# First expert: loads of the tokens' results get an earlier latest time in the list scheduler, and six high parts are cast by DMAs of GpSimd's queue

## The chip, the cores and the metric

The kernel runs on one core of one Trainium2 chip. The metric is device time in microseconds of one execution. All times are those of the profiled execution unless it is said otherwise; a line number such as L882 is a line of the kernel before.

## What is computed

Attention with a tanh cap over 2 x 12 heads of 448 x 64, and then two expert layers over the 896 tokens of 768 features, each with 2048 hidden features. The weights come as 64-bit floats, everything else is 32-bit.

```python
scores = cap * tanh((q @ k.T / sqrt(64)) / cap)
attn = softmax(scores) @ v                    # 2 x 12 x 448 x 64
x = attn.transpose(0, 2, 1, 3).reshape(896, 768)
h = x @ moe_w_in                              # 768 x 2048
g = where(h > 0, h, exp(min(h, 0)) - 1)
x = g @ moe_w_out                             # 2048 x 768
h = maximum(x @ moe2_w_in, 0)
out = (h * h) @ moe2_w_out
```

## The kernel before

**Precision.** Each matmul of 32-bit data is made of three in fp32r: high part by high part, high by low, low by high (`mm`, L487 to L489). So each operand exists twice: a high part, which is a cast, and a low part, which is the operand minus its high part.

**Weights.** SP loads them as 64-bit words into two buffers `raw0` and `raw1`, a couple of pieces at a time. `to_fp32` turns a couple into 32-bit floats in `f0` or `f1`: three ACT steps that read raw (L838, L837, L840), then two on DVE (L842, L844), and for the Strassen stages three more sums on DVE (L849, L852). `piece` then makes a piece's high part by a cast (L876 on ACT, or L877 on DVE, as the scheduler likes) and its low part by a subtraction on DVE (L882). The parts lie in slots: og0/og1, og2/og3, og4/og5 and og6/og7, and for some stages xh/xl; the even one is the high part.

**Stages of the first expert.** The hidden features are worked in four phases. In the first, products with `w_in` are plain (`plain_products`), the function of the hidden layer is made of the accumulators (`evac`: Relu L907, exp L913, L916, then the high and low parts gh and gl, L937 and L943), and six pieces of `w_out` follow (`out1_half`, pieces number 3 to 8, 24 matmuls each, their accumulators copied to yp at L1135). Then come Strassen products (`strassen_quad`), which also need sums of the tokens' blocks, yh and yl. These are made by `yp_sums`: the attention's results, which stand in DRAM as xd0 to xd5, are loaded into yp (L1247), DVE sums them (L1070) into the buffers ep0 to ep3, and high parts yh (L937 or L938) and low parts yl (L943) follow.

**What sets the order.** Attention is written out by hand. From its end on a list scheduler, `Plan`, orders the work, in two plans; the second covers both experts. Each task is added with its engines, a cost, what it reads and writes, and a lag for those who wait for it. PE's tasks keep their order. For each other task `run` works out a latest time backwards from PE's uses, and then each engine takes, among the tasks that are ready when it comes free, the one whose latest time is earliest. The engine queues then run in that order, and a queue whose next instruction waits holds up all that stands behind it. The plan knows of engines DVE, ACT and SP beside PE. The second plan doesn't know of the store of xd5 that attention's last task makes on SP, nor of the memory that yp takes over from attention's buffers.

Of the kernel before, what the change touches and what calls it, by code (L numbers as in the profile page):

```python
# [28 lines left out]
def attention_moe_kernel(  # L29
# [12 lines left out]
    nc = tc.nc  # L42
# [3 lines left out]
    P = 128  # L46
    NFULL = S // P
    LAST = S - NFULL * P
    KC = DM // P
    FC = DFF // P  # L50
    NP = H // 2
    KH = KC // 2
# [438 lines left out]
    def half(t, c, b):  # L491
        return t[:, b, c]

    PE, DVE, ACT, SP = "PE", "DVE", "ACT", "SP"

    def dve(n, fast=False):
        return 0.14 + n / (1920 if fast else 960)

    def act(n):
        return 0.17 + n / 1160  # L500
# [3 lines left out]
    class Plan:  # L504
# [2 lines left out]
        LAG = 0.15  # L507

        def __init__(self):
            self.tasks, self.writer, self.readers = [], {}, {}  # L510

        def add(self, options, reads=(), writes=(), lag=None):

            options = [options] if isinstance(options, tuple) else options
            i = len(self.tasks)
            before = set()
            for r in reads:
                if r in self.writer:
                    before.add(self.writer[r])
            for r in writes:  # L520
                if r in self.writer:
                    before.add(self.writer[r])
                before.update(self.readers.get(r, ()))
            before.discard(i)
            for r in reads:
                self.readers.setdefault(r, set()).add(i)
            for r in writes:
                self.writer[r], self.readers[r] = i, set()
            self.tasks.append((options, before, self.LAG if lag is None else lag))
# [8 lines left out]
        def run(self, free):  # L538
            tasks = self.tasks
            n = len(tasks)  # L540
            after = [[] for _ in tasks]
            for i, (_, before, _) in enumerate(tasks):
                for j in before:
                    after[j].append(i)
            latest, at = [0.0] * n, free[PE]
            for i, (options, _, _) in enumerate(tasks):
                if options[0][0] == PE:
                    latest[i] = at
                    at += options[0][1]
            for i in reversed(range(n)):  # L550
                options, _, lag = tasks[i]
                if options[0][0] != PE:
                    cost = min(o[1] for o in options)
                    latest[i] = min([latest[j] for j in after[i]] + [at + 5.0]) - cost - lag
            waiting = [len(before) for _, before, _ in tasks]
            ready = [0.0] * n
            pe = [i for i, t in enumerate(tasks) if t[0][0][0] == PE]
            queue = {PE: pe[::-1]}
            open_ = {e: [] for e in (DVE, ACT, SP)}

            def opened(i):
                for e, _, _ in tasks[i][0]:
                    if e in open_:
                        open_[e].append(i)

            for i in range(n):
                if not waiting[i]:
                    opened(i)
            order, left, done = [], n, set()
            while left:  # L570
                best = None
                for e in (PE,):
                    if queue[e] and not waiting[queue[e][-1]]:
                        i = queue[e][-1]
                        t = max(free[e], ready[i])
                        if best is None or t < best[0]:
                            best = t, e, i
                for e in (DVE, ACT, SP):
                    if open_[e]:
                        t = max(free[e], min(ready[i] for i in open_[e]))  # L580
                        if best is None or t < best[0]:
                            i = min(
                                (i for i in open_[e] if ready[i] <= t),
                                key=lambda i: (latest[i] + SHY * (e == DVE and len(tasks[i][0]) > 1), i),
                            )
                            best = t, e, i
                t, e, i = best
                options, _, lag = tasks[i]
                cost, fn = next((c, f) for o, c, f in options if o == e)
                if e in queue:  # L590
                    queue[e].pop()
                for q in open_.values():
                    if i in q:
                        q.remove(i)
                free[e] = t + cost
                for j in after[i]:
                    waiting[j] -= 1
                    same = all(o[0] == e for o in tasks[j][0])
                    ready[j] = max(ready[j], t + cost + (0.0 if same and e != SP else lag))
                    if not waiting[j]:  # L600
                        opened(j)
                order.append((t, i, e, cost, fn))
                left -= 1
            self.order = sorted(order, key=lambda o: (o[0], o[1]))
            for _, _, _, _, fn in self.order:
                fn()
            return free
# [24 lines left out]

    PLAIN = 0, 1
    OUT1 = ((0, 0), (1, 0), (0, 1), (1, 1), (2, 0), (2, 1))
    pieces = []
    for ph in range(PH):
        pieces += [
            (in_loads(w_in1, ph * QP + q, j), (ph, q) > PLAIN) for q in range(ph == 0, QP) for j in range(KH)
        ]
        pieces += [(out1_loads(ph, *at), False) for at in OUT1]  # L640
    for ph in range(PH):
# [18 lines left out]
    with tc.manual_schedule():  # L660
# [125 lines left out]
        plan = Plan()  # L786
        counts, slots = dict(piece=0, ep=0, set=1, made=0), list(OGS)
# [66 lines left out]

        def piece():

            k, z = place[counts["piece"]]
            full = couples[k][z][1]
            counts["piece"] += 1
            if k == counts["made"]:  # L860
                to_fp32()
            s = slots.pop(0)
            slots.append(s)
            if s < 4:
                h, l = groups[2 * s], groups[2 * s + 1]
                kh, kl = [("oh", s)], [("ol", s)]
            else:
                h, l = (t[:, 1, :KH].rearrange("p c n -> p (c n)")[:, :7 * P].rearrange(
                    "p (a n) -> p a n", n=P) for t in (xh, xl))
                kh, kl = ([(("x", kc, 1), p) for kc in range(KH)] for p in "hl")  # L870
            n = 7 if full else 4
            src = fs[(k + 1) % 2][:, z, 8 - n - (1 - full) * 4:8 - (1 - full) * 4]
            kf = [(x, k % 2, z) for x in ("f", "fx")]
            add(
                [
                    (ACT, act(n * P), lambda: nc.scalar.copy(h[:, :n], src)),  # L876
                    (DVE, dve(n * P, True), lambda: nc.vector.tensor_copy(h[:, :n], src)),  # L877
                ],
                kf, kh,
            )  # L880
            add(
                (DVE, dve(n * P), lambda: nc.vector.tensor_tensor(  # L882
                    l[:, :n], src, h[:, :n].bitcast(F32), op=ALU.subtract)),
                kf + kh, kl,
            )
            return h, l, kh + kl
# [301 lines left out]
        h, l = split_p_steps(end, 1)  # L1188
# [23 lines left out]
        made = [piece() for _ in range(KH - 1)]  # L1212
        plain_products(s1, range(1), made)
        to_fp32()
        free = plan.run({PE: 3.1, DVE: 2.1, ACT: 0.3, SP: 0.0})
        attn.close()
        gp = ctx.enter_context(tc.tile_pool(name="gp", bufs=1, side="right"))
        yh, yl = (gp.tile([P, 4, KH, S], F32R, name=x) for x in ("yh", "yl"))
# [7 lines left out]
        plan = Plan()  # L1226
# [5 lines left out]
        for ph in range(PH):  # L1232
            if ph:
                if ph == PLAIN[0] + 1:
                    slots.insert(0, 4)
                for q in range(QP):
                    if (ph, q) > PLAIN:
                        strassen_quad(next_set(), ph * QP + q, "elu")
                        continue
                    s = next_set()  # L1240
                    plain_products(s, range(KH))
                    plain_end(s, ph * QP + q, "elu")
            else:
                plain_products(s1, range(1, KH), made + [piece()])
                plain_end(s1, 1, "elu")
                for m in range(KC):
                    add((SP, 0.5, lambda m=m: nc.sync.dma_start(  # L1247
                        yp[:, m].rearrange("p (b s) -> p b s", b=B), xd[m])),
                        [("xd", m)], [("yp", m, b) for b in range(B)], 4.0)
                for j in range(KH):  # L1250
                    yp_sums(j)
            if ph == PH - 1:
                slots.remove(4)
            s = [next_set() for _ in range(KH)]
            for j, fp in OUT1:
                out1_half(s[j], fp)
                if fp:
                    out1_end(s[j], ph, j)
# [49 lines left out]
```

## Time and profile before

| | us |
|---|---|
| median of 3 runs | 569.45 (569.22 to 570.21) |
| the profiled execution | 571.93 |
| its span in the trace | 570.1 |
| PE busy | 561.3 |
| DVE busy | 484.8 |
| ACT busy | 405.7 |
| GpSimd (POOL) busy | 18.3 |

The granted TensorE clock is 1.00 of full speed, 2.4 GHz, in every stretch that was read. Attention ends at about 119 us, the plain products of the first phase of the first expert run to 144.8, the six pieces of `w_out` to 174.0, and Strassen stages follow. An engine's busy time says how much it worked; whether the end moves is read from what PE waits for, since PE is busy in 98% of the span. GpSimd has no work after attention.

### The profile page before, as it was taken

To read this page: it belongs to the slowest core of one execution; us is meant where nothing else is said; L and a number is where in the kernel's file an instruction comes from. 1 tells how busy PE (TensorE), PEld (TensorE's weight loads), DVE (VectorE), ACT (ScalarE), POOL (GpSimd) and SP (SyncE) were. 2 spreads that over 40 slices of the span, in tenths; PEclk is the share of its full clock that TensorE was granted. 3 is DMA by queue.
4 is the path that set the end of the run, shared out by engine and by line. 5 is a ranking of instruction groups with operands and counts; after the bars stand their busy time and mean duration, and the time that the engine had idled before them with its cause. 6 is when DMAs were issued, how large, how long until landed. Compare 5 with 4: busy or idle time off the path is not lost.

```text
span 570.1 us, 7830 instructions
## 1 busy us (share of the span) xinstructions
PE 561.3 (98%) x2940; PEld 491.4 (86%) x2940; DVE 484.8 (85%) x689; ACT 405.7 (71%) x445; POOL 18.3 (3%) x28
## 2 busy tenths in 40 slices
PE   8999999999998999999999999999999999999997
PEld 6777777689997999989999999998999899989985
DVE  6799999897899889989968995998889878987843
ACT  6889999955997994688537786696596369546700
POOL 3211011000000000000000000000000000000000
PEclk9999999999999999999999999999999999999999
DMA  7625444336754244424332333224423424332013
GB/s 188 172 68 158 122 128 142 104 123 212 242 179 129 94 139 156 139 77 158 104 115 75 115 111 144 75 75 148 143 91 124 160 76 135 126 110 74 2 66 129
DMA packets 65974, 70.20 MB, mean 123 GB/s; under 512 B 28544, under 2 KB 47872, under 8 KB 65936
## 3 DMA queue, kind: packets, MB, share of 16 engines
q1 hardware_dynamic: 64560, 69.05, 38.1%
q10 hardware_dynamic: 1344, 0.59, 0.4%
q8 instruction: 23, 0.38, 0.3%
q14 instruction: 15, 0.12, 0.1%
q0 software_dynamic: 32, 0.07, 0.0%
HBM read 64.09 MB, written 5.55 MB: 122 GB/s over the span
## 4 chain that ended last, share of the span: by engine, by line
PE 90%; DVE 6%; ACT 2%; issue 1%; DVEq 0%; ACTq 0%
PE acc L1112 20%; PE acc L489 18%; PE acc L487 18%; PE acc L488 18%; PE po L321 8%; PE sc L265 4%; PE pt L191 1%; DVE pl L297 1%; DVE ph L296 1%; PE sc L219 1%; ACT e L274 0%; DVE f L844 0%; DVE kql L215 0%; DVE yl L943 0%; DVE og L882 0%
## 5 line engine op out<-in xcount | busy, mean ns | idle before, releaser
L1112 PE MATMUL acc<-og,gh 128*128 128x512 f32 (+1 forms) x350 | 86.4, 338 | 0.0
L876 ACT CAST og<-f 128x512 fp32r<-128x512 f32 (+1 forms) x46 | 34.8, 766 | 58.1 <-DVE f L852 18.6
L838 ACT ACTIVATE f<-raw 128x1024 f16<-128x1024 f32 (+1 forms) x47 | 64.1, 1365 | 7.0 <-DMA raw<-in_moe_w_out_dram 3.4
L882 DVE TENSOR_TENSOR og<-f,og 128x512 fp32r<-128x512 f32 (+1 forms) x78 | 63.5, 831 | 5.1 <-ACT og L876 2.4
L489 PE MATMUL acc<-xh,og 128*128 128x448 f32 x180 | 66.2, 368 | 0.3
L1112 PEld LDWEIGHTS acc<-og,gh 128*128 128x128 f32 x350 | 60.3, 190 | 7.0
L488 PE MATMUL acc<-xl,og 128*128 128x448 f32 x180 | 66.0, 366 | 0.0
L487 PE MATMUL acc<-xh,og 128*128 128x448 f32 x180 | 65.9, 366 | 0.0
L487 PE MATMUL acc<-gh,og 128*128 128x448 f32 x176 | 64.5, 367 | 0.0
L488 PE MATMUL acc<-gl,og 128*128 128x448 f32 x176 | 64.5, 367 | 0.0
L489 PE MATMUL acc<-gh,og 128*128 128x448 f32 x176 | 64.5, 367 | 0.0
L840 ACT ACTIVATE f<-raw 128x1024 uint16<-128x1024 uint8 (+1 forms) x47 | 64.3, 1367 | 0.0
L1141 DVE TENSOR_TENSOR yp<-yp,acc 128x448 f32<-128x448 f32 (+2 forms) x69 | 43.4, 638 | 18.9 <-PE acc L1112 14.8
L1112 PE MATMUL acc<-og,gl 128*128 128x512 f32 (+1 forms) x175 | 59.2, 338 | 0.0
L844 DVE SCALAR_TENSOR_TENSOR f<-f 128x1024 uint32<-128x1024 uint32 (+1 forms) x47 | 56.8, 1209 | 1.4 <-ACT f L840 0.6
L837 ACT ACTIVATE f<-raw 128x1024 f32<-128x1024 f32 (+1 forms) x47 | 52.6, 1119 | 0.1
L274 ACT ACTIVATE e<-sc,tsc 128x896 f32<-128x896 f32 (+1 forms) x48 | 43.4, 908 | 0.2 <-PE sc L265 0.2
L487 PE MATMUL acc<-yh,og 128*128 128x448 f32 x112 | 41.4, 370 | 0.0
L489 PE MATMUL acc<-yh,og 128*128 128x448 f32 x112 | 41.0, 367 | 0.0
L488 PE MATMUL acc<-yl,og 128*128 128x448 f32 x112 | 41.0, 366 | 0.0
L297 DVE TENSOR_TENSOR pl<-e,ph 128x1792 fp32r<-128x1792 f32 (+1 forms) x24 | 37.6, 1566 | 1.9 <-DVE ph L296 0.5
L282 ACT ACTIVATE e<-e,capt 128x1792 f32<-128x1792 f32 (+1 forms) x24 | 38.6, 1608 | 0.8
(137 smaller groups left out, 1200.9 us busy)
## 6 DMA issues: line engine op xcount, KB each, us to landing
raw<-in_moe_w_in_dram SPq DMA_DIRECT2D x45, 512.0 KB, 4.4
raw<-in_moe_w_out_dram SPq DMA_DIRECT2D x48, 256.0 KB, 4.1
raw<-in_moe_w_out_dram SPq DMA_DIRECT2D x24, 512.0 KB, 4.3
bc<-far SPq DMA_DIRECT2D x12, 224.0 KB, 3.4
xd<-xn SPq DMA_DIRECT2D x12, 224.0 KB, 2.8
yp<-xd SPq DMA_DIRECT2D x6, 448.0 KB, 6.8
v<-in_v_dram SPq DMA_DIRECT2D x12, 192.0 KB, 3.3
k<-in_k_dram SPq DMA_DIRECT2D x15, 128.0 KB, 3.2
```

Of the source, the lines that this page charges most:

```text
L274: nc.scalar.activation(st["e", n][:, 2 * c:2 * c + w], st["sc", n, c][:, :w, :S], AF.Tanh, scale=tsc)
L321: nc.tensor.matmul(po[:, u, :S], vt[r, at[0]], pt[r, at[1]], start=i == 0 and j < 2, stop=i == 1 and j >= len(mms) - 2,)
L487: nc.tensor.matmul(acc, w[0], x[0], start=first, stop=False, skip_group_check=True)
L488: nc.tensor.matmul(acc, w[0], x[1], start=False, stop=False, skip_group_check=True)
L489: nc.tensor.matmul(acc, w[1], x[0], start=False, stop=last, skip_group_check=True)
L837: add((ACT, act(e) + 0.04 * n, lambda: nc.scalar.activation(a, hi, AF.Abs, scale=2.0 ** 16)), kr, ka)
L838: add((ACT, act(e) + 0.17 * n, lambda: nc.scalar.activation(top, hi, AF.Copy, scale=2.0 ** -100)), kr, kx)
L840: add((ACT, act(e) + 0.17 * n, lambda: nc.scalar.activation(bottom, byte, AF.Copy, scale=1 / 32, bias=-31 / 64)), kr, kx)
L844: add((DVE, dve(e), lambda: nc.vector.scalar_tensor_tensor(out=b, in0=b, scalar=3, in1=q.bitcast(U32), op0=ALU.logical_shift_left, op1=ALU ...
L882: (DVE, dve(n * P), lambda: nc.vector.tensor_tensor(l[:, :n], src, h[:, :n].bitcast(F32), op=ALU.subtract)),
L1112: nc.tensor.matmul(acc, x[:, f, g], w, start=a, stop=z, skip_group_check=True)
L1141: add((DVE, dve(n), lambda: nc.vector.tensor_tensor(to, to, acc(), op=ALU.add)), key + keys, keys)
```

## The change

Two things are changed, both in the stretch from about 130 to 180 us.

The loads of the tokens' results, yp<-xd, are added in another order (0, 3, 1, 4, 2, 5), and each gets an amount `soon` that is taken off its latest time: 30 for the first two, 15 for the next two, 0 for the last two.

For the six pieces of `w_out` in the first phase (`BY_DMA`, pieces 3 to 8), the cast to the high part is no longer a task of ACT or DVE but a DMA of GpSimd's queue, from f0 or f1 to the slot, with a type change on the way. The scheduler gets POOL as a further engine; it counts 0.6 us on the queue and 2.8 us until the cast has landed.

```diff
-                    latest[i] = min([latest[j] for j in after[i]] + [at + 5.0]) - cost - lag
+                    latest[i] = min([latest[j] for j in after[i]] + [at + 5.0]) - cost - lag - self.soon.get(i, 0.0)
...
-            open_ = {e: [] for e in (DVE, ACT, SP)}
+            open_ = {e: [] for e in (DVE, ACT, SP, POOL)}
...
+    BY_DMA = range(3, 9)
...
+            by_dma = counts["piece"] in BY_DMA
...
-            add(
-                [
-                    (ACT, act(n * P), lambda: nc.scalar.copy(h[:, :n], src)),
-                    (DVE, dve(n * P, True), lambda: nc.vector.tensor_copy(h[:, :n], src)),
-                ],
-                kf, kh,
-            )
+            if by_dma:
+                add((POOL, 0.6, lambda: nc.gpsimd.dma_start(h[:, :n], src)), kf, kh, 2.8 if n == 4 else 4.2)
+            else:
+                add(
+                    [
+                        (ACT, act(n * P), lambda: nc.scalar.copy(h[:, :n], src)),
+                        (DVE, dve(n * P, True), lambda: nc.vector.tensor_copy(h[:, :n], src)),
+                    ],
+                    kf, kh,
+                )
...
-                for m in range(KC):
+                for m in (m for j in range(KH) for m in (j, KH + j)):
+                    plan.soon[len(plan.tasks)] = 30 - 15 * (m % KH)
                     add((SP, 0.5, lambda m=m: nc.sync.dma_start(
```

The scheduler's other choices move with these two. Three places stand here; the others differ in kind no more than these. Lines behind the edit count six or seven higher in the new kernel: L907, L913, L916, L937 and L943 are L913, L919, L922, L943 and L949 there, L838, L837 and L840 are L840, L839 and L842.

On SP, at the end of attention's last work (xd5<-xn is its last store), before:

```order
L351 DMA far_1344<-rd_1343 64x14
L352 DMA bc_1345<-far_1344 64x896
L375 DMA xd5_100<-xn_1346 128x448
L655 DMA raw0_72<-in_moe_w_out_dram 128x2x128 x4
L655 DMA raw1_73<-in_moe_w_out_dram 128x2x128 x4
L1247 DMA yp_1510<-xd0_95 128x896
```

and now:

```order
L352 DMA bc_1345<-far_1344 64x896
L375 DMA xd5_100<-xn_1346 128x448
L1254 DMA yp_1510<-xd0_95 128x896
L1254 DMA yp_1510<-xd3_98 128x896
L657 DMA raw0_72<-in_moe_w_out_dram 128x2x128 x4
L657 DMA raw1_73<-in_moe_w_out_dram 128x2x128 x4
```

Two loads of yp stand ahead of the eight loads of weights that feed f1 (raw0) and f0 (raw1).

On ACT, where the hidden function of the last plain accumulators (acc4 to acc7) meets the couple of pieces 4 and 5 in raw0, before:

```order
L937 CAST gh_1504<-ep1_1507 128x896
L838 ACTIVATE f1_1331<-raw0_72 128x2x512
L837 ACTIVATE f1_1331<-raw0_72 128x2x512
L840 ACTIVATE f1_1331<-raw0_72 128x2x512
L907 ACTIVATE ep2_1508<-acc4_1462 128x448
L907 ACTIVATE ep2_1508<-acc5_1463 128x448
```

and now:

```order
L943 CAST gh_1504<-ep1_1507 128x896
L913 ACTIVATE ep2_1508<-acc4_1462 128x448
L840 ACTIVATE f1_1331<-raw0_72 128x2x512
L839 ACTIVATE f1_1331<-raw0_72 128x2x512
L842 ACTIVATE f1_1331<-raw0_72 128x2x512
L913 ACTIVATE ep2_1508<-acc5_1463 128x448
```

The Relu of acc4 moved ahead of the three steps on raw0.

On DVE, from gl of the first hidden features to og5, the low half of piece 4, before:

```order
L943 TENSOR_TENSOR gl_1505<-ep1_1507,gh_1504 128x896
L842 TENSOR_SCALAR f1_1331<-f1_1331 128x2x512
L844 SCALAR_TENSOR_TENSOR f1_1331<-f1_1331 128x2x512
L877 CAST og4_1332<-f1_1331 128x512
L882 TENSOR_TENSOR og5_1333<-f1_1331,og4_1332 128x512
```

and now, from the last of the four sums over yp on:

```order
L1076 TENSOR_TENSOR ep1_1507<-yp_1510,ep0_1506 128x448
L844 TENSOR_SCALAR f1_1331<-f1_1331 128x2x512
L944 CAST yh_1502<-ep0_1506 128x2x448
L846 SCALAR_TENSOR_TENSOR f1_1331<-f1_1331 128x2x512
L922 SCALAR_TENSOR_TENSOR ep2_1508<-ep2_1508,acc5_1463 128x448
L922 SCALAR_TENSOR_TENSOR ep2_1508<-ep2_1508,acc4_1462 128x448
L949 TENSOR_TENSOR yl_1503<-ep0_1506,yh_1502 128x2x448
L922 SCALAR_TENSOR_TENSOR ep3_1509<-ep3_1509,acc7_1465 128x448
L922 SCALAR_TENSOR_TENSOR ep3_1509<-ep3_1509,acc6_1464 128x448
L944 CAST gh_1504<-ep2_1508 128x896
L888 TENSOR_TENSOR og5_1333<-f1_1331,og4_1332 128x512
```

Four sums over yp (the first row is the last of them), a cast of yh and a subtraction of yl moved up here, the cast of og4 is no longer on DVE, a cast of gh came over from ACT, and og5 stands six instructions behind f1's last step, not two. On GpSimd, whose queue held nothing here, the six casts stand in the order of the pieces: og2, og4, og6, og0, og2, og4.

## Rows read from the trace of the kernel before

**Rows 1.** The page, part 1: busy us (share of the span) and instructions of each engine.

```profile
PE 561.3 (98%) x2940; PEld 491.4 (86%) x2940; DVE 484.8 (85%) x689; ACT 405.7 (71%) x445; POOL 18.3 (3%) x28
```

**Rows 2.** PE's waits, whole span: engine line <- releaser: us in total, times, longest us.

```profile
PE acc L489 <- DVE xl L882: 1.3, 1, 1.3
```

**Rows 3.** The timeline, PE, start of first Strassen stage: start us, us, engine line op.

```profile
174.22 0.36 PE L488 MATMUL acc<-xl,xh 128*128 128x448 f32 x1
175.85 0.47 PE L489 MATMUL acc<-xh,xl 128*128 128x448 f32 x1 [1.27 <-DVE xl L882]
176.16 0.36 PE L487 MATMUL acc<-xh,og 128*128 128x448 f32 x1
...
178.16 0.36 PE L487 MATMUL acc<-yh,xh 128*128 128x448 f32 x1
```

**Rows 4.** The timeline, PE: last plain products, then the first two pieces of w_out.

```profile
141.59 0.36 PE L489 MATMUL acc<-xh,og 128*128 128x448 f32 x1
...
144.83 0.36 PE L487 MATMUL acc<-gh,og 128*128 128x448 f32 x1
...
149.70 0.36 PE L487 MATMUL acc<-gh,og 128*128 128x448 f32 x1
...
150.10 0.37 PE L489 MATMUL acc<-gh,og 128*128 128x448 f32 x1
```

**Rows 5.** The timeline, ACT, 140 to 146 us.

```profile
140.80 1.39 ACT L838 ACTIVATE f<-raw 128x1024 f16<-128x1024 f32 x1
...
143.06 1.36 ACT L840 ACTIVATE f<-raw 128x1024 uint16<-128x1024 uint8 x1
144.29 0.93 ACT L907 ACTIVATE ep<-acc 128x448 f32<-128x448 f32 x2
```

**Rows 6.** The timeline, DVE, 139 to 176 us ([idle before <-releaser] at the end).

```profile
139.85 2.16 DVE L943 TENSOR_TENSOR gl<-ep,gh 128x896 fp32r<-128x896 f32 x2
143.19 0.69 DVE L842 TENSOR_SCALAR f<-f 128x1024 f32<-128x1024 f32 x1 [1.18 <-ACT f L837]
144.46 1.23 DVE L844 SCALAR_TENSOR_TENSOR f<-f 128x1024 uint32<-128x1024 uint32 x1 [0.58 <-ACT f L840]
...
146.18 0.69 DVE L882 TENSOR_TENSOR og<-f,og 128x512 fp32r<-128x512 f32 x1
...
148.99 1.15 DVE L916 SCALAR_TENSOR_TENSOR ep<-ep,acc 128x448 f32<-128x448 f32 x2
...
165.01 0.62 DVE L938 CAST yh<-ep 128x896 fp32r<-128x896 f32 x1
...
174.71 1.09 DVE L882 TENSOR_TENSOR xl<-f,xh 128x896 fp32r<-128x896 f32 x1
```

**Rows 7.** The timeline, DMA queue of SP, 132 to 148 us.

```profile
132.68 0.33 SPq L375 DMA_DIRECT2D xd<-xn  x1
133.05 4.05 SPq L655 DMA_DIRECT2D raw<-in_moe_w_out_dram  x8
137.28 0.52 SPq L1247 DMA_DIRECT2D yp<-xd  x1
...
145.38 2.52 SPq L1247 DMA_DIRECT2D yp<-xd  x5
```

**Rows 8.** DMA issues (131:145; then 143:152; then whole span): KB each, median us to landing.

```profile
raw<-in_moe_w_out_dram SPq DMA_DIRECT2D x10, 256.0 KB, 4.6
...
xd<-xn SPq DMA_DIRECT2D x1, 224.0 KB, 1.9
...
yp<-xd SPq DMA_DIRECT2D x5, 448.0 KB, 7.1
...
qz<-in_q_dram POOLq DMA_DIRECT2D x1, 64.0 KB, 2.8
```

**Rows 9.** Windows: us, busy of each engine, PEclk, DMA share, GB/s.

```profile
133.00:143.00 10.00, 10.00 (x51) 9.27 (x50) 7.13 (x12) 7.52 (x10) 0.00 (x0) 1.00 0.84 279
143.00:157.00 14.00, 14.00 (x71) 12.96 (x70) 12.96 (x20) 13.25 (x18) 0.00 (x0) 1.00 0.76 252
```

More of the change, by code (lines that the diff above doesn't have):

```diff
@@ L492, in half @@
         return t[:, b, c]
-    PE, DVE, ACT, SP = "PE", "DVE", "ACT", "SP"
+    PE, DVE, ACT, SP, POOL = "PE", "DVE", "ACT", "SP", "POOL"
     def dve(n, fast=False):
@@ L509, in __init__ @@
         def __init__(self):
-            self.tasks, self.writer, self.readers = [], {}, {}
+            self.tasks, self.writer, self.readers, self.soon = [], {}, {}, {}
         def add(self, options, reads=(), writes=(), lag=None):
@@ L577, in run @@
                             best = t, e, i
-                for e in (DVE, ACT, SP):
+                for e in (DVE, ACT, SP, POOL):
                     if open_[e]:
@@ L598, in run @@
                     same = all(o[0] == e for o in tasks[j][0])
-                    ready[j] = max(ready[j], t + cost + (0.0 if same and e != SP else lag))
+                    ready[j] = max(ready[j], t + cost + (0.0 if same and e not in (SP, POOL) else lag))
                     if not waiting[j]:
@@ L1214, in attention_moe_kernel @@
         to_fp32()
-        free = plan.run({PE: 3.1, DVE: 2.1, ACT: 0.3, SP: 0.0})
+        free = plan.run({PE: 3.1, DVE: 2.1, ACT: 0.3, SP: 0.0, POOL: 0.0})
         attn.close()
```

## Prediction

> **What bounds the kernel now.** Part 1 of the page comes first: PE is busy for 561.3 of 570.1 us [rows 1], so a change can give back only time in which PE waits. The list of PE's waits shows which of them this change can reach: most lie in attention, and one lies in the stretch that the second plan orders, 1.3 us of L489 on the DVE instruction that makes `xl` [rows 2]. The timeline of PE shows what it costs in all. L488 of the first Strassen product starts at 174.22, L489 only at 175.85, and the eighth matmul start after that L488 is at 178.16 [rows 3]. Eight steps took 3.94 us. Undisturbed, 24 steps take 149.70 - 144.83 = 4.87 us [rows 4], 0.203 each, so eight take 1.62: **2.3 us** are lost. The cause is DVE's queue, which reaches the subtraction into `xl` at 174.71 [rows 6], after PE wanted it. Earlier DVE stood idle: 1.18 and 0.58 us before the two steps on f1 at 143.19 and 144.46 [rows 6]. The change wants to fill such gaps with the sums over yp, and takes casts off DVE and ACT.
>
> **The profiled execution** took 571.93 us (span 570.1), 2.48 above the median of 569.45. I work out a difference on the trace and add it to both alike.
>
> **Part 1: the old wait.** From the end of f1's step at 144.46 + 1.23 = 145.69 DVE needs 29.0 us to reach `xl` at 174.71 [rows 6]. In the new order six, no longer ten, L1070 sums stand in that piece, the casts of og4, og6 and og0 are gone, one cast of yh goes to ACT, one subtraction of yl falls behind `xl`, and three casts or copies (gh, yp, xh) come over from ACT. With 0.62 for a cast of 896 [rows 6], about the same for a sum and a copy, 1.08 for one subtraction of 896 (half of the 2.16 at 139.85) and 0.49 for a small cast (it lay between 145.69 and the subtraction at 146.18), that is -4 x 0.62 - 3 x 0.49 - 0.62 - 1.08 + 3 x 0.62 = -3.8 us. So even if f1 is ready 2 us later, DVE reaches `xl` at about 173, ahead of PE. The 2.3 us go: **-2.3**.
>
> **Part 2: what is late next.** The second piece of w_out (og4, og5) is due on PE at 149.70, its low half og5 with the first L489 at 150.10 [rows 4]. Before, cast and subtraction followed f1 at once and the subtraction began at 146.18 [rows 6], 3 us early. Now three things stand in between, and I add them up.
>
> (a) ACT. The new order puts the Relu of acc4 ahead of the three steps on raw0. That bank's last matmul, the sixteenth before 144.83, starts at 141.59 and takes 0.36 [rows 4], so ACT, free at 140.80 before [rows 5], stands until 141.99 and spends 0.46 (half of 0.93) on it: the steps on raw0 start at 142.45, not 140.80. From the first one's start to the last one's end they took 143.06 + 1.36 - 140.80 = 3.62 us [rows 5]: end 146.07, 1.65 later than before.
>
> (b) SP. yp<-xd now stands twice ahead of raw0. yp takes the memory that attention leaves, and xd5's store reads from it, so SP waits for that store: issued at 132.68 [rows 7], landing 1.9 later [rows 8], 134.6. Two yp loads and four quarters of raw0 are then 2 x 0.459 + 4 x 0.262 = 1.97 MB; at 279 GB/s, the rate of this stretch [rows 9], 7.1 us: landed at 141.7, against 142.45 when ACT asks. No cost, with 0.7 us of margin. At the yp loads' own 7.1 us to landing [rows 8] it would be later than that.
>
> (c) GpSimd's DMA. f1's last step ends at 146.07 + 0.04 + 1.23 = 147.34 and the cast of og4 is issued at 147.4. How long such a DMA takes, no row shows: 262 KB, SBUF to SBUF, with a change of type, beside SP's loads. The bounds are 2.8 us (the one load from GpSimd's queue, 64 KB, in an almost idle start) and 7.1 us (yp<-xd, 448 KB, in these very microseconds) [rows 8]. I take the nearer row, GpSimd's own, 2.8, and add the other 0.197 MB at 252 GB/s [rows 9], 0.78 us, twice, because the engines are already 76% busy there with SP's transfers [rows 9]: **4.4 us**. og4 lands at 151.8, the subtraction takes 0.69 [rows 6], and L489 starts at about 152.55, not 150.10: 2.45 us, and 0.1 more as PE starts up again (from 175.85 to 176.16 the step was 0.31, not 0.20 [rows 3]): **+2.55**.
>
> The Trainium skill (DMA: Bandwidth & Descriptors, section Anatomy of one DMA — SWDGE (gpsimd) path) gives for a DMA of GpSimd's queue about 2.0 us and the bytes at 436 GB/s. For 262 KB that is an estimate from that page of 2.6 us; the sum would then end at the floor below, 569.2. No row here shows a cast by DMA, so the runs have to decide.
>
> A floor holds even for a fast DMA. Ahead of og5, DVE's queue now has ep2 twice (1.15 [rows 6]), yl (1.08), ep3 twice (1.15) and the cast of gh (0.62): 147.34 + 4.0 = 151.3, og5 ready at 152.0, L489 at 152.05, a loss of 2.05. Below that no speed of the cast leads.
>
> (d) Behind and beside. og3's subtraction waits for og2's cast, issued when PE has done with that slot, 48 matmuls or 9.7 us before 144.83 [rows 4], at 135.1, and landed at 139.5; DVE comes to it at 139.85, where gl stood [rows 6], and needs gl, two subtractions later, by 145.0. Hidden, but the two gl and four L1070 sums behind it (2.16 + 4 x 0.62) reach to about 145, and then two more instructions to 146.1, just when ACT is ready: an og2 that lands later than about 139.8 pushes f1 back by the same. A slow cast counts **twice**. The four casts that follow have more room: PE takes 4.87 us a piece, and each is issued over 5 us ahead of its use.
>
> Casts off ACT and DVE (six of about half a microsecond) are worth nothing by themselves: apart from the two places above PE waits for neither.
>
> **Sum.** -2.3 + 2.55 = +0.2 us: 572.1 on the profiled execution, **569.6** as a median.
>
> **Rivals.**
> *The cast is slow.* One mechanism: og2 late, so f1 late, then og4 late. L489 starts at 147.4 + 0.75 + L + (L - 4.6) for a cast of L us above 4.6. It is over 0.2% slower, stall over 3.4, from L = 4.9. At 5.5 it is 154.55: 4.45 + 0.1 - 2.3 = +2.2, **571.7**; at 7.1 it is 157.75, +5.4, 574.9. For it: yp<-xd at 7.1 beside it [rows 8]; against it: the 2.8 of GpSimd's own row, and a quarter of the engines' time idle. A late raw0 (b) adds its lateness to the same chain. Chance 0.3 with what goes with it.
> *The new wait is hidden* and the old one gone: 569.45 - 2.3 = **567.1**. It would need L489 by 150.10, so a cast under 1.9 us and none of the DVE rows ahead of og5. The floor speaks against it; it remains if ACT or DVE run ahead of what I read, or if the gaps in DVE are worth more than I see. Chance 0.1.
> *The change does not do what it says*, DVE is still late at `xl` and both waits stand: 569.45 + 2.5 = 572.0. PE reaches that place 2.5 us later itself, so this needs DVE to lose over 6 us. Chance 0.03, counted with the slow cast.
>
> **How the numbers follow.** The forecast, one wait for another, has 0.6; its own range is 569.2 (floor) to 570.5 (L near 4.9). About 0.2%, 1.1 us, is what a measurement of this kernel can tell from no change: 568.3 to 570.6 is the same. So faster 0.1, same 0.6, slower 0.3. The range leaves out the hidden wait and casts over 5.5 us: 568.7 to 571.8.
>
> **What would show it.** PE's waits: L489 on `xl` gone; a new wait of 2 to 2.6 us near 150 on og5's DVE line, at the first piece whose weights are og4 and og5. ACT's Relu of acc4 ahead of the steps on raw0, waiting for PE at about 141. GpSimd's DMAs with 3.4 to 5 us to landing. DVE's `xl` at about 173 with PE there at 176.5. I am wrong if og5 ends before 150, if raw0 lands after 142.5, or if the casts take under 3 or over 5 us.

## The result and the profile after

The changed kernel takes 576.49 us (median of 4 runs, 574.16 to 578.06) where the kernel before takes 569.83 (4 runs, 569.22 to 570.50): ratio 1.0113, 95% interval 1.0073 to 1.0154, so 1.1% slower. The forecast was 569.6 with a range of 568.7 to 571.8. The profiled execution took 578.06 us, its span is 575.9.

Pieces are counted from 0, as in `BY_DMA`: piece 3 is the first of w_out, piece 4 the second (the prediction's og4 and og5).

PE's waits, whole span (engine line <- releaser: us in total, times, longest): the old wait [rows 2] is gone, a longer one stands at the first product of piece 4.

```profile
PE acc L487 <- DMA og<-f: 5.1, 1, 5.1
```

The timeline of PE at that place, against [rows 4] (start us, us, engine line operation, [idle before <- releaser]):

```profile
143.67 0.36 PE L487 MATMUL acc<-gh,og 128*128 128x448 f32 x1
...
148.33 0.37 PE L489 MATMUL acc<-gh,og 128*128 128x448 f32 x1
153.79 0.71 PE L487 MATMUL acc<-gh,og 128*128 128x448 f32 x1 [5.09 <-DMA og<-f]
154.30 0.58 PE L488 MATMUL acc<-gl,og 128*128 128x448 f32 x1
154.67 0.58 PE L489 MATMUL acc<-gh,og 128*128 128x448 f32 x1
...
159.41 0.37 PE L487 MATMUL acc<-gh,og 128*128 128x448 f32 x1
```

Three losses are to be read here: 5.26 us beyond the usual step between 148.33 and 153.79; 0.31 as PE starts up again; and steps of 0.37 instead of 0.20 us until 159.1, about 2.3 us in all. The windows give the reason for the last (us, busy of PE, PEld, DVE, ACT and POOL, PEclk, DMA share, GB/s):

```profile
148.00:154.00 6.00, 0.91 (x5) 0.55 (x4) 2.37 (x5) 5.64 (x7) 0.00 (x0) 0.87 0.98 293
154.00:160.00 6.00, 6.00 (x18) 5.32 (x19) 5.97 (x9) 1.53 (x2) 1.04 (x2) 0.56 1.04 387
```

PE stood for 5.1 us, and behind that the granted clock was at half (1.2 instead of 2.4 GHz) for most of the second window; 18 matmuls ran where before, in the same window, it was 31.

Who made PE wait: the timeline shows when GpSimd's queue issues the casts and when SP issues its loads beside them, and the DMA issues of 144:150 say how long each took (KB each, median us to landing).

```profile
128.86 0.56 POOL L878 DMA_DIRECT2D og<-f  x1 [30.24 <-DVE f L846]
146.79 1.06 POOL L878 DMA_DIRECT2D og<-f  x2 [17.37 <-DVE f L846]
```

```profile
144.93 0.88 SPq L657 DMA_DIRECT2D raw<-in_moe_w_out_dram  x2
145.86 1.41 SPq L1254 DMA_DIRECT2D yp<-xd  x3
```

```profile
yp<-xd SPq DMA_DIRECT2D x3, 448.0 KB, 7.7
raw<-in_moe_w_out_dram SPq DMA_DIRECT2D x2, 256.0 KB, 3.1
og<-f POOLq DMA_DIRECT2D x2, 256.0 KB, 7.6
```

The cast of piece 3 was issued at 128.86, with much less beside it; the DMA issues of 126:140 have it:

```profile
og<-f POOLq DMA_DIRECT2D x1, 256.0 KB, 2.3
```

So the same 256 KB took 2.3 us there and 7.6 here; that is the median of two, the cast of piece 4 landed 6.9 us and the one of piece 5 8.3 us after its issue. That it was the company of SP's loads is what the experiments had to show.

### The profile page after: what moved, and what is told of

Its sections match the earlier page's. It is cut to its first block, busy times and chain, and to the rows that moved or that the text cites. A ratio compares the mean times of both kernels' runs of the same rounds, so it can differ in the third digit from the quotient of the medians.

```text
span 575.9 us, 7845 instructions
## 1 busy us (share of the span) xinstructions
PE 564.2 (98%) x2940; PEld 494.6 (86%) x2940; DVE 484.5 (84%) x687; ACT 403.2 (70%) x441; POOL 21.4 (4%) x34
## 4 chain that ended last, share of the span: by engine, by line
PE 94%; DVE 2%; ACT 2%; DMA 1%; issue 1%; POOLq 0%; ACTq 0%; DVEq 0%
PE acc L1118 20%; PE acc L487 19%; PE acc L489 19%; PE acc L488 19%; PE po L321 9%; PE sc L265 5%; PE pt L191 2%; DMA og<-f 1%; PE sc L219 1%; ACT e L274 0%; DVE pl L297 0%; DVE ph L296 0%; ACT e L282 0%; ACT f L840 0%; ACT f L842 0%
## 5 line engine op out<-in xcount | busy, mean ns | idle before, releaser
L882 ACT CAST og<-f 128x512 fp32r<-128x512 f32 (+1 forms) x44 | 33.5, 774 | 56.2 <-PE acc L488 17.8
L487 PE MATMUL acc<-gh,og 128*128 128x448 f32 x176 | 66.0, 375 | 5.1 <-DMA og<-f 5.1
L840 ACT ACTIVATE f<-raw 128x1024 f16<-128x1024 f32 (+1 forms) x47 | 64.2, 1366 | 6.8 <-DMA raw<-in_moe_w_out_dram 3.0
L489 PE MATMUL acc<-xh,og 128*128 128x448 f32 x180 | 66.1, 367 | 0.0
L487 PE MATMUL acc<-xh,og 128*128 128x448 f32 x180 | 66.1, 367 | 0.0
L488 PE MATMUL acc<-gl,og 128*128 128x448 f32 x176 | 65.8, 374 | 0.0
L489 PE MATMUL acc<-gh,og 128*128 128x448 f32 x176 | 65.7, 373 | 0.0
L842 ACT ACTIVATE f<-raw 128x1024 uint16<-128x1024 uint8 (+1 forms) x47 | 64.2, 1365 | 0.0
L839 ACT ACTIVATE f<-raw 128x1024 f32<-128x1024 f32 (+1 forms) x47 | 52.6, 1120 | 0.8 <-DVE og L888 0.8
L487 PE MATMUL acc<-yh,og 128*128 128x448 f32 x112 | 41.4, 370 | 0.0
L487 PEld LDWEIGHTS acc<-gh,og 128*128 128x128 f32 x176 | 33.8, 192 | 8.7 <-issue 5.4
L489 PE MATMUL acc<-yh,og 128*128 128x448 f32 x112 | 41.1, 367 | 0.0
```

Of the source, the lines that this page charges most:

```text
L487: nc.tensor.matmul(acc, w[0], x[0], start=first, stop=False, skip_group_check=True)
L488: nc.tensor.matmul(acc, w[0], x[1], start=False, stop=False, skip_group_check=True)
L489: nc.tensor.matmul(acc, w[1], x[0], start=False, stop=last, skip_group_check=True)
L839: add((ACT, act(e) + 0.04 * n, lambda: nc.scalar.activation(a, hi, AF.Abs, scale=2.0 ** 16)), kr, ka)
L840: add((ACT, act(e) + 0.17 * n, lambda: nc.scalar.activation(top, hi, AF.Copy, scale=2.0 ** -100)), kr, kx)
L842: add((ACT, act(e) + 0.17 * n, lambda: nc.scalar.activation(bottom, byte, AF.Copy, scale=1 / 32, bias=-31 / 64)), kr, kx)
```

## A sum that holds for all profiles

PE is busy in 98% of the span before [rows 1], so I split each span into three parts. **Gaps**: between 130 and 200 us, for each matmul step over 0.235 us, what it has beyond 0.203 (waits, restarts, half clock; in e6 also 24 added matmuls, 4.9). **Long step**: in stretches of some executions the step of the 128x448 matmuls is 0.2067 instead of 0.2027, at a granted clock that reads 1.00 for both; over such stretches 0.004 a step is summed. **Rest**: the span less both.

```
kernel                          span   gaps  long step  rest
before                          570.1   2.5     2.8     564.8
before again (e5)               567.7   2.4     1.9     563.5
after                           575.9   7.9     4.4     563.6
after again (e9)                573.7  10.1     0.0     563.7
e1 early loads only             568.9   2.2     2.5     564.2
e2 casts only                   572.4   8.2     0.7     563.5
e3 results' loads apart         573.5   6.1     3.8     563.7
e4 all loads apart              573.3   9.1     0.3     563.9
e6 no idle                      572.3   8.5     0.2     563.7
e7 pieces 4, 5 on engines       570.9   4.3     2.4     564.3
e12 the same again              573.5   7.1     2.6     563.8
e8 late casts only              570.6   4.7     2.5     563.4
e10 results' loads all early    569.3   4.6     0.7     564.0
e11 third piece only            569.7   2.8     3.0     564.0
```

The rest is 563.4 to 564.3 for thirteen of the fourteen, and 564.8 in the first profile of before, whose attention ended 1 us later than in the second. What the change does to the time is in the gaps of these 70 us; the long step comes and goes with the execution, in the kernel before as well.

## The experiments

The kernel before was run beside each group of experiments: its median was 569.15 us beside e1 to e4, 569.58 beside e5 to e8 and 570.51 beside e9 to e12. Each ratio is against those runs and is not the quotient of the two medians. Piece numbers are counted from 0, so "the fourth and fifth piece" of an expectation are pieces 4 and 5, but "the ninth piece" is piece 8.

**e1: the early loads alone.**

```
-    BY_DMA = range(3, 9)
+    BY_DMA = ()
```

> No high part is cast by a DMA; the lower latest time for the loads of the tokens' results is kept. Theory S (shared DMA engines: the cast of the fourth piece takes long because SyncE's loads run beside it; its lateness costs a wait of 5.1 us and then half the clock): without the casts the loads alone cost nothing, no wait on a DMA at the fourth piece, a wait for xl of 1 to 2 us is back; 568.5 to 570.0 us. Rival L (the moved loads are the cost, by holding up the raw loads or the queue): 573 us or more, with TensorE still late around 153. Open beside both: if the matmul pitch of 0.2067 from 159 on comes with the half clock, it is 0.2027 here until about 240, as before.

Measured: 568.68 us beside 569.15, ratio 0.9994 (0.9969 to 1.0019): no difference. The waits list has no DMA in this stretch, and a shorter old wait:

```profile
PE acc L489 <- DVE xl L888: 0.8, 1, 0.8
```

Theory L, the moved loads as the cost, falls.

**e2: the casts alone.** The loads of results as before the change:

```
-    for m in (m for j in range(KH) for m in (j, KH + j)):
-        plan.soon[len(plan.tasks)] = 30 - 15 * (m % KH)
+    for m in range(KC):
```

> Six high parts are cast by DMAs of GpSimd's queue, the loads of the tokens' results go where they went before the change. Theory S: the casts of the fourth and fifth piece are issued at about 146 beside two raw loads and all six loads of results (before: 252 GB/s in that stretch), land 6 to 8 us after issue, TensorE waits 3 to 5 us, the clock falls to 0.50 behind that; the wait for xl is gone; 572 to 575 us. Rival L (the moved loads are the cost): 567.0 to 569.0 us, the cast landing in 2.3 to 3 us.

Measured: 575.49 us, ratio 1.0104 (1.0060 to 1.0148), half a microsecond above theory S's range. Nearly the whole loss sits in the casts. DMA issues of 144:150, then PE's waits:

```profile
yp<-xd SPq DMA_DIRECT2D x5, 448.0 KB, 9.1
og<-f POOLq DMA_DIRECT2D x2, 256.0 KB, 8.1
```

```profile
PE acc L487 <- DMA og<-f: 4.2, 1, 4.2
```

**e3 and e4: the casts without the loads.** In e3 the last three loads of results wait for piece 5's low part (a one-column memset of each yp slice, which the load overwrites, holds them); in e4 the two raw loads of piece 8 as well (the lines that hold the loads; the rest of the edit is left out).

```
+    for m in (KH + 1, 2, KH + 2):                       # behind piece 5
+        add((DVE, 0.14, lambda m=m: nc.vector.memset(yp[:, m, :1], 0.0)),
+            pk, [("yp", m, b) for b in range(B)])
+        yp_load(m, 15 if m % KH == 1 else 0)
     elif k:
+        if k == 4:                                      # e4 only
+            add((DVE, 0.14, lambda: nc.vector.memset(
+                raw[:, 0, 0, :1].bitcast(U32), 0)), ends[0], kr)
         add((SP, 2.9 * n, load), [], kr, 1.5)
```

> As the changed kernel, but the last three loads of the tokens' results are made to wait for the fifth piece's low part, so that 1.4 MB less moves beside the casts of the fourth and fifth piece; the two raw loads still do. Theory S: some 1.5 MB instead of 2.9 MB at about 390 GB/s, the cast of the fourth piece lands 3.5 to 4.5 us after its issue instead of 6.8, the wait of 5.1 us falls to 1.5 to 3 us, and the time to 570.5 to 573.5 us. Rival V (the cast's own descriptors are late, because VectorE is busy then or because two casts stand in the queue): landing 6 us or more, wait about 5 us, 575 to 578 us.

> As the run before it, but the two raw loads of the ninth piece wait for the fifth piece's low part too: of SyncE's transfers none starts beside the two casts. Theory S: the two casts share the engines with each other alone, the first lands 2.3 to 4.4 us after issue, TensorE waits 0 to 2 us, the clock stays at 1.00; later waits for the delayed loads may take up to 1 us; 568.5 to 571.5 us. Rival V: landing 6 us or more, 575 to 578 us.

Measured: e3 575.59 us (573.07 to 576.76, 5 runs), e4 576.48. Both times lie above what theory S said (up to 573.5 and 571.5) and in theory V's range, so the totals alone would speak for V. The landings speak against it. DMA issues of e3 and of e4, 144:150:

```profile
raw<-in_moe_w_out_dram SPq DMA_DIRECT2D x2, 256.0 KB, 2.8
og<-f POOLq DMA_DIRECT2D x2, 256.0 KB, 2.4
```

```profile
og<-f POOLq DMA_DIRECT2D x2, 256.0 KB, 2.4
```

2.4 us in both (median of two casts), with VectorE at work in the same microseconds and two casts in the queue: theory V falls. In e3 the two raw loads still run beside the casts (they land at 147.7 and 148.4, the first cast at 149.2), so here it is the loads of results that stretch a cast to 7 or 8 us. Theory S had e3's landing at 3.5 to 4.5, too long. The timeline of PE in e3 shows what is left with a fast cast:

```profile
148.35 0.37 PE L489 MATMUL acc<-gh,og 128*128 128x448 f32 x1
149.35 0.44 PE L487 MATMUL acc<-gh,og 128*128 128x448 f32 x1 [0.63 <-DMA og<-f]
149.63 0.37 PE L488 MATMUL acc<-gl,og 128*128 128x448 f32 x1
150.85 0.47 PE L489 MATMUL acc<-gh,og 128*128 128x448 f32 x1 [0.86 <-DVE og L888]
```

Up to the L489 that is 1.9 us beyond the usual steps. Later e3 waits again, 1.0 us for the cast of piece 6 and 1.1 for a yl, and e4, whose raw data come late, for a low part (waits of e4):

```profile
PE acc L489 <- DVE og L892: 4.2, 3, 2.9
PE acc L487 <- DMA og<-f: 1.2, 1, 1.2
```

So in e4 the rivals' times can't be told by the total: its delayed loads cost what the early cast gave. e3's profiled execution took its median, 575.59; beside the second profile of before (569.53) it has 3.7 us more of gaps and 1.9 more of long step, which accounts for 5.6 of the 6.1 us. Whether its other executions had as much of the long step was not seen.

**e5: the kernel before, once more.**

> The kernel before, for a second profile of it. The pitch of the 128x448 matmuls (start to start) was 0.2027 up to about 243 and 0.2067 from there to about 370 in its first profile, 0.2027 from 185 on in the profile with the casts alone. Theory P (the longer pitch comes and goes with the execution, and makes the runs of one kernel differ by up to 3 us): another place or length of the stretch here, and the time goes with it: about 568.5 us without it, 571.5 us with 145 us of it. Rival Q (it belongs to the program): again from 243 to 370, 571 to 572 us.

Measured: 569.53 us (one run). Theory P holds: the long step is there, in another place. Two windows of this run; at the short step 40 us hold 199 or 200 matmuls, at the long one 195 or 196:

```profile
200.00:240.00 40.00, 40.00 (x195) 36.32 (x195) 36.13 (x53) 28.24 (x30) 0.00 (x0) 1.00 0.44 143
250.00:290.00 40.00, 40.00 (x200) 37.05 (x199) 38.15 (x58) 28.72 (x30) 0.00 (x0) 1.00 0.46 149
```

In the first profile of the same kernel the two windows are the other way round:

```profile
200.00:240.00 40.00, 40.00 (x199) 37.07 (x199) 36.81 (x54) 29.38 (x31) 0.00 (x0) 1.00 0.43 139
250.00:290.00 40.00, 40.00 (x196) 36.32 (x195) 37.60 (x57) 28.87 (x29) 0.00 (x0) 1.00 0.43 142
```

**e6: no idle time.**

```
+    for _ in range(24):     # into the bank that piece 4's first product overwrites
+        nc.tensor.matmul(bank(4 * s + 1), w[:, 0], gpart(gh, 0, 1),
+                         start=True, stop=True, ...)
```

> As the changed kernel, with 24 matmuls more (128x448, 24 times 0.2027 = 4.9 us) just ahead of the fourth piece's first product, into the bank that this product overwrites: TensorE works through the wait for the cast. Theory W (half the clock follows from the idle 5 us): the wait on the cast is under 1 us, the granted clock stays at 1.00 up to 165, the first product starts at about 154 as before, and the matmuls behind it come at 0.20 instead of 0.37 us: 2.6 us less, 573.5 to 574.5 us. Rival: the clock falls all the same (what lowered it isn't the idle time): 576 to 577.5 us.

Measured: 573.80 us (9 runs, 572.08 to 579.37), ratio 1.0086 (1.0058 to 1.0114). That is 4.2 above its own runs of before, where the changed kernel lay 6.7 and, in e9, 6.4 above its own: 2.2 to 2.4 us less, though the intervals overlap. PE's timeline:

```profile
149.24 5.23 PE L1053 MATMUL acc<-gh,og 128*128 128x448 f32 x24 [0.67 <-DVE ep L922]
156.51 0.47 PE L487 MATMUL acc<-gh,og 128*128 128x448 f32 x1 [2.05 <-DMA og<-f]
156.82 0.36 PE L488 MATMUL acc<-gl,og 128*128 128x448 f32 x1
```

The total lands as theory W put it, and the clock too: granted 1.00 from 148 to 165, steps of 0.20 behind the first product. That product starts 2.7 us later than in the changed kernel, since raw0 landed later in this execution (ACT waited 2.31 us for it), and PE still waits 2.05 us for the cast where theory W had under 1. So that the total agrees is partly luck; what this profile shows is that with 2.05 us of idle time in place of 5.09 the half clock didn't come.

**e7 and e12: the casts of pieces 4 and 5 back on the engines.**

```
-    BY_DMA = range(3, 9)
+    BY_DMA = 3, 6, 7, 8
```

> As the changed kernel, but the casts of the fourth and fifth piece (those that land beside the loads, and whose f is ready last) go to ScalarE or VectorE again; the other four stay DMAs. Theory S: the wait of 5.1 us and the half clock are gone, waits of up to 0.7 us at the fourth and fifth piece on the engines' casts and 1.5 us on xl stay: 568.5 to 570.5 us. Rival: the four other casts cost too (each holds its product by its own latency): 572 us or more.

> The kernel with the casts of the fourth and fifth piece on the engines again: its gaps between 130 and 200 were 1.8 us above those of before, its median 4.5 us. Theory G: gaps of 4 to 5 us again and 571 to 573 us, the first median having been raised by executions with a long stretch of the 0.2067 pitch. Rival: gaps of 6 us or more in this execution, the casts of the sixth to eighth piece landing later, and 573.5 to 575 us again.

Measured: 574.13 and 574.01 us, ratios 1.0083 and 1.0053. Theory S of e7 expected 568.5 to 570.5; its rival, that the four other casts cost too, had 572 or more and was right, and so was e12's rival (gaps of 6 us or more, 573.5 to 575). PE's waits in this stretch, of e7 and of e12:

```profile
PE acc L489 <- DVE xl L888: 1.6, 1, 1.6
PE acc L487 <- DVE ep L922: 0.6, 1, 0.6
```

```profile
PE acc L489 <- DVE xl L888: 2.5, 1, 2.5
PE acc L487 <- DVE ep L922: 1.1, 1, 1.1
```

No DMA is waited for, and the 5.1 us are gone, as expected. But the old wait is longer than before (1.3 [rows 2]), and it differs by 0.9 us between two executions of one kernel; in e12 the half clock came behind it, gaps 7.1 instead of 4.3. Some executions of these kernels pay more than one profile shows. What makes DVE late at `xl` can be read from its timeline: the low parts of pieces 6 and 7 wait in its queue for the casts by DMA, which were issued at about 155 and landed 5.2 to 6.8 us later (e7, then e12):

```profile
160.17 0.69 DVE L888 TENSOR_TENSOR og<-f,og 128x512 fp32r<-128x512 f32 x1 [1.89 <-DMA og<-f]
161.59 0.69 DVE L888 TENSOR_TENSOR og<-f,og 128x512 fp32r<-128x512 f32 x1 [0.73 <-DMA og<-f]
```

```profile
160.30 0.69 DVE L888 TENSOR_TENSOR og<-f,og 128x512 fp32r<-128x512 f32 x1 [1.78 <-DMA og<-f]
162.43 0.69 DVE L888 TENSOR_TENSOR og<-f,og 128x512 fp32r<-128x512 f32 x1 [1.44 <-DMA og<-f]
```

That is 2.6 and 3.2 us of DVE's time. It reaches `xl` at 176.54 and 177.28, where e1, with no cast by DMA, reaches it at 173.96: 2.6 and 3.3 us later. So a cast by DMA holds up not only PE but also DVE, through the subtraction that stands behind it in DVE's queue.

**e8: two late casts only**, on the kernel before (loads of results as in e2, `BY_DMA = 6, 7`).

> The kernel before with one thing changed: the casts of the sixth and seventh piece alone (counted from 0: numbers 6 and 7) go as DMAs of GpSimd's queue, the loads of results as before. VectorE or ScalarE is rid of 2 casts ahead of the wait for xl (1.3 us long before), TensorE needs these pieces only after 160. Theory S (a cast by DMA pays where its operand is ready early): the wait for xl falls below 0.5 us, no wait on a DMA: 567.0 to 569.0 us, 0.1 to 0.4% less than before. Rival: their landing of 4.4 us beside the raw loads of that stretch makes the product wait, 569.5 to 571 us.

Measured: 571.75 us, ratio 1.0031 (1.0015 to 1.0046). The rival was right in kind (its upper end was 571): the two casts landed after 6.6 us (median), beside raw loads of 512 KB, and PE waits for the first of them, DVE 3.2 us for the same one, while the wait on `xl` shrinks by 0.2 only:

```profile
PE acc L489 <- DVE xl L888: 1.1, 1, 1.1
PE acc L487 <- DMA og<-f: 0.9, 1, 0.9
```

**e9: the changed kernel, once more.**

> The changed kernel, for a second profile. Theory G (span = a base equal in all these kernels, plus TensorE's gaps between 130 and 200, plus what the longer pitch costs; the ten profiles so far give a base of 562.5 to 563.9 us): gaps of 7 to 9 us again (a wait of 4.5 to 6 us for the fourth piece's cast, the clock at 0.50 for some 6 us behind it), pitch in another place; span 563.3 + gaps + pitch within 1 us. Rival: the gaps differ by more than 2 us from execution to execution (the cast's landing depends on how the loads' packets fall), so that one profile doesn't speak for the median of 576.5 us.

Measured: 576.95 us beside 570.51, ratio 1.0116. The wait is 6.7 us this time, the cast landed after 8.4, the clock was at 0.50 behind it (waits; DMA issues of 144:150; window):

```profile
PE acc L487 <- DMA og<-f: 6.7, 1, 6.7
```

```profile
og<-f POOLq DMA_DIRECT2D x2, 256.0 KB, 8.4
```

```profile
154.00:160.00 6.00, 4.28 (x12) 3.76 (x13) 4.39 (x6) 1.84 (x3) 0.00 (x0) 0.50 0.88 311
```

Theory G's sum holds; so does its rival's point, gaps 2.2 us larger than in the first profile.

**e10: all loads of results early.**

```
-    plan.soon[len(plan.tasks)] = 30 - 15 * (m % KH)
+    plan.soon[len(plan.tasks)] = 30
```

> As the changed kernel, but all six loads of the tokens' results get the lowest latest time (30 us off for each), so that the last three go out at about 139 instead of 146 and nothing but the two raw loads runs beside the casts of the fourth and fifth piece. Theory S: these casts land in 2.2 to 3.0 us instead of 6.8 to 7.6, TensorE waits 0.5 to 1.2 us for the fourth piece's cast and up to 0.9 us for its low part, the clock stays at 1.00, no wait for xl; gaps of 3 to 4.5 us: 570.0 to 573.0 us. Rival: the four loads ahead of the seventh piece's raw loads make those late: a new wait on an f, 574 us or more.

Measured: 571.73 us, ratio 1.0039 (1.0012 to 1.0066): with all six casts still DMAs, moving three loads from 146 to 137 to 139 gives back 5.2 of the 6.4 us that e9 lost beside the same runs of before. DMA issues of 144:150 and waits:

```profile
raw<-in_moe_w_out_dram SPq DMA_DIRECT2D x2, 256.0 KB, 4.2
og<-f POOLq DMA_DIRECT2D x2, 256.0 KB, 4.1
```

```profile
PE acc L487 <- DMA og<-f: 3.1, 2, 2.5
```

The time and the clock, 1.00, are as theory S said. The landing, 4.1, lies above its 2.2 to 3.0, and the wait for the cast of piece 4, 2.5, above its 0.5 to 1.2: the loads of results now stand ahead of the last four quarters of the raw loads, which landed up to 149.0, and two more raw loads followed up to 146.5, so some of SP's loads still ran beside the casts.

**e11: the cast of piece 3 only** (`BY_DMA = 3,`).

> As the changed kernel, but of the six casts only the first stays a DMA (piece 3, issued at about 129 and landed 2.3 us later with no load beside it, its product at 145). Theory S (a cast by DMA costs nothing where its operand is ready well ahead): like the early loads alone (568.7 us), plus up to 0.6 us at the fourth piece: 568.3 to 570.0 us. Rival F (every kernel with casts on GpSimd's queue pays a fixed 2 us or more, whatever their place, as the median of 574.1 us with four casts suggests): 570.5 to 572.5 us.

Measured: 571.28 us beside 570.51, ratio 1.0001 (0.9969 to 1.0034). The median lies in F's range, but the runs of before beside it are 1.4 us longer than those beside e1, and against them F's 2 us (1.0035) lie just outside the interval; so this speaks for theory S, by a small margin. The old wait is gone here, and the time not: a wait at piece 4 has come in its place.

```profile
PE acc L487 <- DVE ep L922: 1.0, 1, 1.0
```

No version here is faster than the kernel before; e1 and e11 equal it.

## Why the prediction was wrong, step by step

**Part 1, the old wait goes:** right in its effect, wrong in its reason. DVE was to reach `xl` at about 173; it reached it at 177.35, since it stood for the casts itself, 3.63 us ahead of the subtraction at 153.68 and 1.14 us for the cast of piece 6. The working took three casts off DVE and had no term for DVE waiting for them. The wait is gone because PE comes later still, at 181.5.

**(a) ACT and f1:** right. The timeline of ACT has the Relu of acc4 first, with the wait for PE that was forecast, then the steps on raw0:

```profile
140.83 0.54 ACT L913 ACTIVATE ep<-acc 128x448 f32<-128x448 f32 x1 [1.33 <-PE acc L489]
141.27 1.39 ACT L840 ACTIVATE f<-raw 128x1024 f16<-128x1024 f32 x1
```

In this execution attention ended 1.16 us earlier (143.67 against 144.83 [rows 4]), so 141.27 answers to 142.43; 142.45 was forecast. DVE's last step on f1 and the subtraction behind the cast:

```profile
144.94 1.23 DVE L846 SCALAR_TENSOR_TENSOR f<-f 128x1024 uint32<-128x1024 uint32 x1
...
153.68 0.69 DVE L888 TENSOR_TENSOR og<-f,og 128x512 fp32r<-128x512 f32 x1 [3.63 <-DMA og<-f]
```

f1 ends at 146.17, which answers to 147.33; 147.34 was forecast.

**(b) the early loads cost nothing:** right in the total, by e1, and ACT doesn't wait for raw0 above. But the margin was smaller than the 0.7 us of the forecast: raw0's last quarter landed at 141.04, 0.2 us before ACT read it, and in e4, e11, e12 and e6 ACT waited 0.5 to 2.3 us for raw0.

**(c) the cast's landing is the step that failed.** Forecast 4.4 us; the cast of piece 4 was issued at 146.79, 0.6 us behind f1 where 0.06 was reckoned, landed 6.9 us later, and let the first product start at 153.79. In e9 it landed after 8.1. The lower bound of 2.8 was too high for a cast with little beside it (2.3), the upper one of 7.1 too low for e9, and the choice between them was wrong: the load from GpSimd's own queue was the nearer row by queue, the load of results the nearer one by place and time. The working counted the company as a share of engine time (76% busy) and added 0.78 us for it. A better count takes all bytes that are in flight together: two raw loads, three loads of results and two casts, 2 x 0.262 + 3 x 0.459 + 2 x 0.262 = 2.4 MB from 144.93 on; at the 293 GB/s of the window they end 8.3 us later, at 153.2. That is a reckoning after the event, and its agreement with the landing at 153.7 is partly luck, since it counts transfers that landed behind it (the second cast at 155.6, the last load at 155.8). But e3, e4 and e10 move the same way: with fewer bytes beside it the cast lands earlier. The Trainium skill (DMA: Bandwidth & Descriptors, section Anatomy of one DMA — SWDGE (gpsimd) path) gave an estimate of 2.6 us: it is near the casts with little beside them, 2.3 and 2.4, and far from those beside the loads of results, 6.9 to 8.1.

The place of the wait was wrong too: the forecast had PE wait at the first L489, for og5. But the first L487 reads og4 itself, due at 149.70 and by the forecast's own landing, 151.8, not there; that is where PE waited.

What (c) cost in all is 7.9 us where 2.55 was forecast: 5.26 of wait, 0.31 of starting up, and 2.3 of half clock, for which the forecast had no term.

**The floor for a fast cast,** a loss of 2.05 us through DVE's queue, held in the main: e3 lost 1.9 up to that L489, and there DVE came to og5 at 150.11, when the cast had landed at 149.21.

**(d) a slow cast counts twice:** wrong. Piece 3's cast was issued at 128.86, not 135.1, as its f and its slot were free by then, and no one waited for it. So the rival "the cast is slow" had the direction and the long landing, but its 574.9 us at 7.1, 5.4 above before, came from a second delay that didn't happen, while the one that did had no term: the half clock behind an idle PE, 2.3 us in the first profile and 2.5 in the second. That 5.4 is also the difference of the gaps in the first pair of profiles is luck.

**The sum as measured:** gaps of 7.9 and 10.1 us against 2.5 and 2.4, that is +5.4 and +7.7 in the two pairs, where +0.2 was forecast; the medians differ by 6.7 and 6.4.

## What to carry to other kernels

A DMA in place of an engine's instruction cost nothing here only where its operand was ready well ahead of its use (e11), and no version here was faster. Its landing is to be reckoned with all bytes that are in flight beside it, not from how it lands alone (2.3 us against 6.9 to 8.1 here). Look for everyone who reads the result: the engine that was to be relieved stands in its own queue for it too. When a wait grows to several microseconds on a PE that was busy without a break, add a term for the half clock behind it. Before one profile is compared with another, sum up PE's gaps and its steps apart: two executions of the changed kernel differed by 4.4 us in steps alone (4.4 and 0.0 of long step).

## What was not expected of the hardware

- The step of the same 128x448 matmuls is 0.2027 or 0.2067 us in stretches of up to 220 us, at a granted clock that reads 1.00 for both (246 to 372 and two short ones in one profile of the kernel before, 178 to 246 and three short ones in the other; none in e9). It was worth 0 to 4.4 us a profile. What sets it stays open.
- A cast of 256 KB from SBUF to SBUF took 2.3 us with little beside it and 6.9 to 8.7 us beside three or five loads of 448 KB.
- Behind waits of 4.2 to 6.7 us PE ran at a granted clock of 0.50 for 3 to 6 us; behind e10's 2.5 us it did not, behind e12's, of 2.5 as well, and e4's 2.9 it did. So the length of the wait alone doesn't decide it; what does stays open.
